# A fused attention and gated feed-forward kernel on one core: four blocks in every slot from the 22nd on, and the last output block in two halves

## The chip, the core and the metric

The kernel runs on one core of a Trainium2 chip. The metric is the device time of one execution in microseconds (us). Three runs of the kernel before the change gave 404.66, 405.2 and 404.98 us; their median is 404.98 us. The profile and the trace come from a further execution, which took 405.6 us.

## The reference, cut to what matters

Inputs q, k and v are float32 of shape (8 batches, 8 heads, 576 tokens, 64). Attention is computed twice and added: once over keys, queries and values averaged in groups of four tokens (144 of them), whose result is repeated four times, and once over a band in which a token sees only the keys less than 4 away. The sum, with the heads side by side, is x, 4608 tokens by 512. Then comes a gated feed-forward layer:

```python
out_up = np.repeat(sm_attn(q_d, k_d, v_d), 4, axis=2)      # q_d, k_d, v_d: means of 4 tokens
scores = np.where(abs(pos[:, None] - pos[None, :]) < 4, scale * q @ k.T, -1e9)
x = (out_up + softmax(scores) @ v)                         # as (4608, 512)
y = (np.maximum(x @ w_gate, 0) * (x @ w_val)) @ w_out      # 512 -> 1536 -> 512
```

## The kernel before, in words

**Two kinds of work are interleaved by hand.** The attention is done in 32 pairs of heads (pair p is two heads of batch p // 4). The feed-forward layer is cut into 9 chunks of 512 tokens. A chunk has twelve **h blocks** (`ffn_h`, 8 matmuls of 128x512 at line 588, then a Relu on ScalarE at line 596 and a product on VectorE at line 598 that makes the tile g) and four **y blocks** (`ffn_y`, 12 matmuls of 128x512 at line 604 into one PSUM bank, a copy to `y_sb` by ScalarE at line 612; `store_y` then issues the store from SyncE's queue, SP, at line 618).

**The list of blocks.** All of them stand in one list, `ffn`, three h blocks and then one y block of the chunk before, over and over, with the four y blocks of the last chunk at the end. `ffn_do` takes the first of the list. If it is an h block whose chunk needs tokens of a batch that isn't finished yet (`made`, the count of finished pairs, is too small), the call does nothing: a *blocked* call.

**The slots.** `slot(n)` for n from -2 to 33 writes out, in program order, the stages of several pairs and up to five calls of `ffn_do`; every engine then runs its own instructions in that order. For n from 14 on, in program order (line numbers of what is timed):

1. SP queue: the DMA transpose of the attention weights of pair n-1 (`turn_a`, line 505, tile `at`), of q and k of pair n+2 (`turn_qk`, line 268), loads of q and k of a pair five ahead (line 180) and of v of pair n+4 (lines 191 and 218), then the stores of finished y blocks.
2. The scores of pair n: TensorE (PE) at lines 336 and 353; VectorE (DVE) adds the mask (389), takes the maximum (411) and subtracts it (412, tile `sm`), and takes the maxima of the pooled scores (395, 396); ScalarE (ACT) the exponentials (448, 436). GpSimd (POOL) sums q and k in fours (323, 326).
3. First call of `ffn_do`.
4. Outputs of pair n-2 on PE: `u_ps` at line 532 and `o_ps` at 555, which read `at`; ACT copies `o_ps` (563). DVE does the sums and weights of pair n (453, 455, 460), and only then the addition that writes the tokens of pair n-2 into `xT` (`add_x`, line 572), after which `made` grows by one. POOL normalises the pooled weights (487).
5. Second call of `ffn_do`, casts on ACT and POOL, then the third and the fourth call, and the fifth where there is one.

Pair p of a batch fills the quarter p % 4 of the features of `xT`; the matmuls of an h block go through the quarters in order, so the fourth of each group of four reads what the last pair of the batch wrote. The matmul outputs `s_ps` (two), `h_ps` (two for each h block), `u_ps` (two), `o_ps` and `y_ps` take six PSUM banks in turn.

**The quota**, the number of calls, is 4 in even slots and 5 in odd ones from slot 14 to the end. Followed through the list, slots 22 to 33 make 54 calls, of which three are blocked: the first of slot 29 (chunk 6 waits for pair 27), the last of slot 32 and the first of slot 33 (chunk 7 waits for pair 31). After slot 33, 32 blocks are left and run one after the other; this is the tail.

Of the kernel before, what the change touches and what calls it, by code (L numbers as in the profile page):

```python
# [41 lines left out]
def _dap(t_ap: bass.AP, extra_off: int, dims) -> bass.AP:  # L42
    return bass.AP(tensor=t_ap.tensor, offset=t_ap.offset + extra_off, ap=list(dims))
# [3 lines left out]
def kernel(  # L47
# [10 lines left out]
    nc = tc.nc  # L58
# [3 lines left out]
    DM = H * D  # L62
    DF = w_gate.shape[1]
    NTOK = B * S
    TCH = 512
    NCH = NTOK // TCH
    NJJ = DF // 128
# [17 lines left out]
    wo_sb = wpool.tile([128, NJJ, DM], FP16, name="wo_sb")  # L85
# [54 lines left out]
    def bank(shape, name, dt=FP32):  # L140
        return psum.tile(shape, dt, name=name, tag="bank")


    def load_h_weights(i):
        cols = slice(384 * i, 384 * i + 384)
        for src, dst in ((w_gate, wg_sb), (w_val, wv_sb)):
            nc.gpsimd.dma_start(
                dst[:, :, cols],
                _dap(src, 384 * i, [[DF, 128], [128 * DF, 4], [1, 384]]),
            )  # L150

    def load_y_weights(i):
        nc.gpsimd.dma_start(
            wo_sb[:, 3 * i : 3 * i + 3, :],
            _dap(w_out, 3 * i * 128 * DM, [[DM, 128], [128 * DM, 3], [1, DM]]),
        )
# [4 lines left out]
    def load(p):  # L161
        off = 2 * p * S * D
        nat = p_nat.tile([96, 2, 768], FP32, name="nat", tag="nat")
        if p < NPE:


            t = nat.rearrange("p a c -> p (a c)").rearrange("p (b h c) -> p b h c", b=3, h=2)
            for src, r0, r1, blk, g0 in (
                (q, 0, 96, 0, 0),
                (q, 0, 48, 1, 96),  # L170
                (k, 48, 96, 1, 0),
                (k, 0, 96, 2, 48),
            ):
                nc.sync.dma_start(  # L174
                    t[r0:r1, blk],
                    _dap(src, off + 4 * g0 * D, [[4 * D, r1 - r0], [S * D, 2], [1, 4 * D]]),
                )
        else:
            for i, src in ((0, q), (1, k)):
                nc.sync.dma_start(  # L180
                    nat[:, i].rearrange("p (h j d) -> p h j d", h=2, j=6),
                    _dap(src, off, [[D, 96], [S * D, 2], [96 * D, 6], [1, D]]),
                )
        st[p] = dict(nat=nat)

    def load_v(p):
        off = 2 * p * S * D
        vst = v_t[p % NV]

        def win(rows, lo, par, w, nw):  # L190
            nc.sync.dma_start(
                vst[64 * par + lo : 64 * par + lo + rows, w : w + nw, :],
                _dap(
                    v,
                    off + (32 * (2 * w + par) - 3 + lo) * D,
                    [[D, rows], [64 * D, nw], [1, D]],
                ),
            )


        if p == 0:
            win(48, 0, 0, 1, NW - 1)
            win(45, 3, 0, 0, 1)
        else:
            win(48, 0, 0, 0, NW)
        if p == NP - 1:
            win(48, 0, 1, 0, NW - 1)
            nc.vector.memset(vst[96:VR, NW - 1, :], 0.0)
            win(35, 0, 1, NW - 1, 1)
        else:  # L210
            win(48, 0, 1, 0, NW)
        st[p]["vst"] = vst
# [40 lines left out]
    def cast_qk_act(p):  # L253
        cast_qk(p, 0)
# [174 lines left out]
    def exp_d(p, h):  # L429
        s = st[p]  # L430
        if h == 0:
            s["ed"] = p_ed.tile([80, 4, S // 4], FP16, name="ed", tag="ed")
            s["sd"] = p_st.tile([80, 4], FP32, name="sd", tag="sd")
        for c in range(2):
            i = 2 * h + c
            nc.scalar.activation(  # L436
                out=s["ed"][:, i, :],
                in_=s["dp"][h][:, c, :],
                func=AF.Exp,
                scale=SCALE / 16.0,  # L440
                bias=s["nb"][:, i : i + 1],
                accum_out=s["sd"][:, i : i + 1],
            )
# [136 lines left out]
    gts = {}  # L580
    ysb = []

    def ffn_h(c, jj):
# [14 lines left out]
        nc.vector.tensor_tensor(out=g, in0=r, in1=h2, op=ALU.mult)  # L598
        gts.setdefault(c, []).append(g)

    def ffn_y(c, ty):
        y = bank([128, DM], "y_ps")
        for jj in range(NJJ):
            nc.tensor.matmul(  # L604
                out=y,
                lhsT=gts[c][jj][:, bass.ts(ty, 128)],
                rhs=wo_sb[:, jj, :],
                start=(jj == 0),
                stop=(jj == NJJ - 1),
            )  # L610
        y_sb = p_y.tile([128, DM], FP32, name="y_sb", tag="y")
        nc.scalar.copy(out=y_sb, in_=y)  # L612
        ysb.append((c * TCH + ty * 128, y_sb))

    def store_y():
        while ysb:
            row, y_sb = ysb.pop(0)
            nc.sync.dma_start(_dap(out, row * DM, [[DM, 128], [1, DM]]), y_sb)

# [9 lines left out]
    def ffn_do():  # L631
        if ffn:
            t = ffn[0]
            if t and t[0] == "h" and made[0] < 4 * (min((t[1] + 1) * TCH - 1, NTOK - 1) // S + 1):
                return
            ffn.pop(0)
            if t:
                (ffn_h if t[0] == "h" else ffn_y)(t[1], t[2])
# [5 lines left out]
    def at_stage(p, *fs, pe=None):  # L644
        if 0 <= p < NP and (pe is None or pe == (p < NPE)):
            for f in fs:
                f(p)
# [5 lines left out]
    loaded = [0]  # L653

    def slot(n):
        quota = 0 if n < 4 else 3 if n < 14 else 5 if n % 2 else 4
        at_stage(n - 1, turn_a, pe=False)
        at_stage(n + 2, turn_qk, pe=False)
        while loaded[0] < min(NP, n + (5 if n < NPE - 2 else 6)):
            load(loaded[0])  # L660
            if loaded[0] < NPE:
                load_v(loaded[0])
            loaded[0] += 1
        at_stage(n + 4, load_v, load_v4, pe=False)
        store_y()
        at_stage(n, scores, scores_d)
        at_stage(n - 1, turn_en_pe, pe=True)
        at_stage(n, pool_v, mask_l, shift_l, copy_vd, exp_l, max_d)
        if n == 0:
            cast_qk_act(1)  # L670
        at_stage(n + 2, cast_qk_pool, pe=True)
        if n + 2 < NPP:
            at_stage(n + 2, cast_v, pe=True)
        at_stage(n + 1, pool_qk, pe=False)
        if n < 4 or n >= NPE:
            at_stage(n + 1, turn_qk_pe, pe=True)
        if quota > 1:
            ffn_do()
        if 4 <= n < NPE:
            at_stage(n + 1, turn_qk_pe, pe=True)  # L680
        at_stage(n - 1, turn_ad_pe, pe=True)
        at_stage(n, lambda p: exp_d(p, 0))
        at_stage(n - 1, outputs, pe=True)
        at_stage(n - 2, outputs, pe=False)
        at_stage(n, sums, weights_l)
        at_stage(n - 1, x_stage, pe=True)
        at_stage(n - 2, x_stage, pe=False)
        at_stage(n, lambda p: exp_d(p, 1))
        if n != -1:
            at_stage(n + 2, cast_qk_act, pe=True)  # L690
        if quota:
            ffn_do()
        if n + 2 >= NPP:
            at_stage(n + 2, cast_v, pe=True)
        at_stage(n + 1, pool_qk, pe=True)
        at_stage(n, weights_d)
        at_stage(n + 3, cast_qk_act, cast_qk_pool, pe=False)
        at_stage(n + 2, cast_v, sum_v4, pe=False)
        if 1 <= n < 5:
            load_h_weights(n - 1)  # L700
        elif 5 <= n < 9:
            load_y_weights(n - 5)
        if quota > 2:
            ffn_do()
        if quota > 3:
            ffn_do()
        if quota > 4:
            ffn_do()

    with tc.manual_schedule():  # L710
        for n in range(-2, NP + 2):
            slot(n)
        while ffn:
            ffn_do()
            store_y()
# [30 lines left out]
```

## Time and profile before

| | |
|---|---|
| median of three runs | 404.98 us (404.66 to 405.2) |
| the profiled execution | 405.6 us |
| its span, first to last instruction | 403.8 us |
| PE busy in the span | 373.0 us (92%) |
| DVE, ACT, POOL busy | 255.9, 206.0, 198.5 us |
| slot 22 begins (first scores of pair 22) | 210.96 us |
| slot 29 begins and ends | 282.88 and 298.94 us |
| PE's last matmul ends | 399.85 us |
| last copy of y on ACT begins | 399.91 us, 0.58 us long |

The span is a little shorter than the execution's time, by 1.8 us here; what lies around it is not in the trace. A row of the timeline gives start, length, engine, line and operation, and in brackets how long its engine was idle just before and what ended that. In the table of stretches, each engine has its busy time and its number of instructions, then the granted clock of PE (1.00 is full speed), the DMA share and the GB/s moved.

### The profile page before, as it was taken

The page shows a single profiled execution, that of the slowest core. Times are in us where ns is not written, and L with a number is a line of the kernel's source. Part 1 is how long each engine was busy: PE and PEld are TensorE (multiplying, and loading weights), DVE is VectorE, ACT ScalarE, POOL GpSimd, SP SyncE. Part 2 cuts the span into 40 slices and gives each one's busy share as a digit, 9 for nine tenths or more (in the row PEclk, how much of TensorE's full clock was granted, in tenths as well). Part 3 has the DMA queues.
Part 4 walks back from the last instruction along what each step waited for, and adds up shares of the span by engine and source line. Part 5 has one row for each costly group of instructions (what it writes and reads, how often), then busy time and mean ns, then how long its engine had stood idle before and what let it go on. Part 6 is the DMA issues. An engine that isn't in the chain of part 4 may idle for free.

```text
span 403.8 us, 11560 instructions
## 1 busy us (share of the span) xinstructions
PE 373.0 (92%) x4544; PEld 192.4 (48%) x4544; DVE 255.9 (63%) x640; ACT 206.0 (51%) x580; POOL 198.5 (49%) x248
## 2 busy tenths in 40 slices
PE   2699897898999999999999999999599999999996
PEld 2587465555544444444444444444244444444442
DVE  4788789878688868775767676777647532222210
ACT  3577577767575555555555555545335422332321
POOL 5587587755668776757475766564551100000000
PEclk9999999989899999999999999999799999999999
DMA  8999999997999999999999999999322100100112
GB/s 195 228 206 216 217 215 234 223 205 164 204 197 194 231 214 204 221 229 204 221 236 228 209 210 201 206 208 197 86 58 58 55 28 26 54 26 26 45 42 97
DMA packets 172059, 65.78 MB, mean 163 GB/s; under 512 B 152726, under 2 KB 165478, under 8 KB 172006
## 3 DMA queue, kind: packets, MB, share of 16 engines
q1 hardware_dynamic: 165830, 60.18, 75.9%
q0 software_dynamic: 5824, 4.72, 7.7%
q8 instruction: 35, 0.57, 0.6%
q10 hardware_dynamic: 352, 0.16, 0.2%
q14 instruction: 18, 0.15, 0.1%
HBM read 48.52 MB, written 9.44 MB: 144 GB/s over the span
## 4 chain that ended last, share of the span: by engine, by line
PE 71%; DMA 9%; DVE 8%; ACT 5%; issue 3%; SPq 2%; POOL 1%; POOLq 0%; ACTq 0%
PE h_ps L588 40%; PE y_ps L604 23%; DMA vst<-in_v_dram 8%; PE s_ps L336 2%; DVE sm L412 2%; PE u_ps L532 2%; DVE s_ps L389 1%; DVE mx L411 1%; PE d_ps L353 1%; SPq L174 1%; PE o_ps L555 1%; DMA nat<-in_k_dram 1%; DVE g L598 1%; ACT ed L436 1%; ACT r L596 1%
## 5 line engine op out<-in xcount | busy, mean ns | idle before, releaser
L598 DVE TENSOR_TENSOR g<-r,h_ps 128x512 f16<-128x512 f16 x108 | 73.9, 684 | 96.6 <-PE h_ps L588 75.2
L588 PE MATMUL h_ps<-xT,wg_sb 128*128 128x512 f16 x432 | 114.9, 388 | 5.5 <-DVE xT L572 4.5
L588 PE MATMUL h_ps<-xT,wv_sb 128*128 128x512 f16 x432 | 114.2, 388 | 0.2
L604 PE MATMUL y_ps<-wo_sb,g 128*128 128x512 f16 x432 | 99.2, 381 | 0.2 <-DVE sm L412 0.2
L596 ACT ACTIVATE r<-h_ps 128x512 f16<-128x512 f32 x108 | 64.3, 596 | 48.7 <-PE h_ps L588 48.4
L588 PEld LDWEIGHTS <-wv_sb 128*128 128x128 f16 x432 | 43.1, 100 | 59.6 <-issue 11.4
L604 PEld LDWEIGHTS <-g 128*128 128x128 f16 x432 | 41.8, 98 | 50.5 <-issue 1.4
L487 POOL TENSOR_TENSOR wts<-ed,rd 80x288 f16<-80x288 f16 x40 | 25.8, 664 | 76.4 <-ACT h L249 24.5
L588 PEld LDWEIGHTS <-wg_sb 128*128 128x128 f16 x432 | 39.1, 99 | 45.9 <-issue 2.9
L612 ACT COPY y_sb<-y_ps 128x512 f32<-128x512 f32 x36 | 21.0, 583 | 62.3 <-PE y_ps L604 62.1
L448 ACT ACTIVATE e<-sm 96x456 f16<-96x456 f32 x32 | 18.6, 583 | 57.1 <-DVE sm L412 57.0
L436 ACT ACTIVATE ed<-d_ps,nb 80x144 f16<-80x144 f32 x128 | 47.5, 380 | 0.0
L262 POOL CAST v<-vst 112x1152 f16<-112x1152 f32 x32 | 37.0, 1158 | 12.7 <-DMA vst<-in_v_dram 10.4
L323 POOL TENSOR_TENSOR t<-qkT 128x576 f32<-128x576 f16 x27 | 30.9, 1143 | 7.4 <-DVE qkT L293 7.4
L389 DVE TENSOR_TENSOR s_ps<-s_ps,mask_sb 96x228 f32<-96x228 f32 x64 | 22.1, 390 | 16.0 <-PE s_ps L336 16.0
L251 POOL CAST h<-nat 96x768 f16<-96x768 f32 x35 | 29.3, 836 | 5.4 <-DMA nat<-in_k_dram 4.8
L572 DVE TENSOR_TENSOR xT<-u_ps,od 128x288 f16<-128x288 f32 x64 | 26.0, 446 | 5.0 <-ACT od L563 5.0
L395 DVE TENSOR_REDUCE d_ps<-d_ps 80x2 f32<-80x288 f32 x64 | 28.9, 452 | 0.0
L412 DVE TENSOR_TENSOR sm<-s_ps,mx 96x228 f32<-96x228 f32 x64 | 25.1, 392 | 2.2
L249 ACT CAST h<-nat 96x768 f16<-96x768 f32 x29 | 24.2, 839 | 4.2 <-DMA nat<-in_k_dram 4.2
L436 ACT ACTIVATION_READ_ACCUMULATOR ed<-d_ps,nb 80x1 f32 x128 | 26.2, 204 | 0.0
L460 DVE TENSOR_TENSOR wts<-e,rl 96x456 f16<-96x456 f16 x32 | 24.8, 776 | 1.1
(53 smaller groups left out, 373.7 us busy)
## 6 DMA issues: line engine op xcount, KB each, us to landing
vst<-in_v_dram SPq DMA_DIRECT2D x62, 216.0 KB, 4.9
out_dram<-y_sb SPq DMA_DIRECT2D x36, 256.0 KB, 3.6
nat<-in_q_dram SPq DMA_DIRECT2D x20, 288.0 KB, 4.2
nat<-in_k_dram SPq DMA_DIRECT2D x20, 288.0 KB, 4.3
v<-in_v_dram SPq DMA_DIRECT2D x40, 144.0 KB, 4.4
nat<-in_q_dram SPq DMA_DIRECT2D x12, 192.0 KB, 7.2
nat<-in_k_dram SPq DMA_DIRECT2D x12, 192.0 KB, 5.1
wg_sb<-in_moe_w_gate_dram POOLq DMA_DIRECT2D x4, 384.0 KB, 8.6
```

Source lines behind the costliest of these rows:

```text
L251: nc.gpsimd.tensor_copy(out=dst, in_=src)
L262: nc.gpsimd.tensor_copy(out=s["v16"], in_=s.pop("vst"))
L323: nc.gpsimd.tensor_tensor(out=t1, in0=qkv[:, :, :, 0], in1=qkv[:, :, :, 1], op=ALU.add)
L389: nc.vector.tensor_tensor(out=sp, in0=sp, in1=mask_sb, op=ALU.add)
L395: nc.vector.tensor_reduce(out=nbr, in_=s["dp"][h], axis=AX.X, op=ALU.max)
L412: nc.vector.tensor_tensor(out=sm[:, half, :], in0=sp, in1=mx[:, half, None].to_broadcast([96, 6, 38]), op=ALU.subtract,)
L436: nc.scalar.activation(out=s["ed"][:, i, :], in_=s["dp"][h][:, c, :], func=AF.Exp, scale=SCALE / 16.0, bias=s["nb"][:, i : i + 1], accum_o ...
L572: nc.vector.tensor_tensor(out=x5[:, :, par], in0=up[par].rearrange("p l (t f) -> p l t f", f=4), in1=od4[:, :, par, :, None].to_broadcast( ...
L588: nc.tensor.matmul(out=h, lhsT=w[:, kk, bass.ts(jj, 128)], rhs=xT[:, kk, bass.ts(c, TCH)], start=(kk == 0), stop=(kk == 3),)
L596: nc.scalar.activation(out=r, in_=h1, func=AF.Relu)
L598: nc.vector.tensor_tensor(out=g, in0=r, in1=h2, op=ALU.mult)
L604: nc.tensor.matmul(out=y, lhsT=gts[c][jj][:, bass.ts(ty, 128)], rhs=wo_sb[:, jj, :], start=(jj == 0), stop=(jj == NJJ - 1),)
```

## The change

The fifth call of `ffn_do` is made only in odd slots up to 21, so slots 22 to 33 all make four calls. Followed through the list, none of the 48 calls is blocked any more, each slot holds three h blocks and one y block, in the order h, (outputs), h, y, h, and 35 blocks are left for the tail.

The y block of the last 128 tokens is computed in two halves of 256 columns: 12 matmuls of 128x256 and a copy by ACT, then 12 more into a second bank and a copy by DVE. Each half has a store of its own. All other y blocks are as before.

```diff
     def ffn_y(c, ty):
-        y = bank([128, DM], "y_ps")
-        for jj in range(NJJ):
-            nc.tensor.matmul(
-                out=y,
-                lhsT=gts[c][jj][:, bass.ts(ty, 128)],
-                rhs=wo_sb[:, jj, :],
-                start=(jj == 0),
-                stop=(jj == NJJ - 1),
-            )
+        row = c * TCH + ty * 128
+        last = row + 128 == NTOK
         y_sb = p_y.tile([128, DM], FP32, name="y_sb", tag="y")
-        nc.scalar.copy(out=y_sb, in_=y)
-        ysb.append((c * TCH + ty * 128, y_sb))
+        for i in range(2 if last else 1):
+            cols = slice(i * DM // 2, (i + 1) * DM // 2) if last else slice(0, DM)
+            y = bank([128, cols.stop - cols.start], "y_ps")
+            for jj in range(NJJ):
+                nc.tensor.matmul(
+                    out=y,
+                    lhsT=gts[c][jj][:, bass.ts(ty, 128)],
+                    rhs=wo_sb[:, jj, cols],
+                    start=(jj == 0),
+                    stop=(jj == NJJ - 1),
+                )
+            if i:
+                nc.vector.tensor_copy(out=y_sb[:, cols], in_=y)
+            else:
+                nc.scalar.copy(out=y_sb[:, cols], in_=y)
+            ysb.append((row, cols, y_sb))
...
-        quota = 0 if n < 4 else 3 if n < 14 else 5 if n % 2 else 4
+        quota = 0 if n < 4 else 3 if n < 14 else 5 if n < 22 and n % 2 else 4
```

`store_y` takes the columns with the row and stores them alone.

More of the change, by code (lines that the diff above doesn't have):

```diff
@@ L601, in ffn_y @@
     def ffn_y(c, ty):
-        y = bank([128, DM], "y_ps")
-        for jj in range(NJJ):
-            nc.tensor.matmul(
-                out=y,
-                lhsT=gts[c][jj][:, bass.ts(ty, 128)],
-                rhs=wo_sb[:, jj, :],
-                start=(jj == 0),
-                stop=(jj == NJJ - 1),
-            )
-        y_sb = p_y.tile([128, DM], FP32, name="y_sb", tag="y")
-        nc.scalar.copy(out=y_sb, in_=y)
-        ysb.append((c * TCH + ty * 128, y_sb))
+        row = c * TCH + ty * 128
+        last = row + 128 == NTOK
+        y_sb = p_y.tile([128, DM], FP32, name="y_sb", tag="y")
+        for i in range(2 if last else 1):
[14 more added lines that the diff above has]
+            ysb.append((row, cols, y_sb))
     def store_y():
         while ysb:
-            row, y_sb = ysb.pop(0)
-            nc.sync.dma_start(_dap(out, row * DM, [[DM, 128], [1, DM]]), y_sb)
+            row, cols, y_sb = ysb.pop(0)
+            n = cols.stop - cols.start
+            nc.sync.dma_start(
+                _dap(out, row * DM + cols.start, [[DM, 128], [1, n]]), y_sb[:, cols]
+            )
     ffn = []
```

## The prediction

> **What bounds the kernel now.** The page first: PE is busy 92% of the span, and the slices show where it isn't.
>
> ```profile
> PE   2699897898999999999999999999599999999996
> ...
> PEclk9999999989899999999999999999799999999999
> DMA  8999999997999999999999999999322100100112
> ```
>
> A slice is 10.1 us. From the eleventh on PE is full but for the last and the 29th (282.7 to 292.8 us), where its clock falls too. So from slot 22 on time is won or lost only where PE stands still or runs slow. Next, the stretches between the first scores of one pair and of the next (slots 22, 23, 25, 28, 29 and 30):
>
> ```profile
> 210.96:220.32 9.36, 9.36 (x126) 4.38 (x126) 7.23 (x19) 5.25 (x17) 4.69 (x7) 1.00 1.24 221
> 220.32:231.45 11.13, 11.09 (x134) 5.17 (x133) 7.91 (x20) 5.97 (x18) 8.16 (x11) 1.00 1.30 216
> ...
> 240.65:252.69 12.04, 11.15 (x134) 5.17 (x133) 8.00 (x20) 6.09 (x18) 8.79 (x11) 1.00 1.24 215
> ...
> 273.68:282.88 9.20, 9.20 (x126) 4.39 (x125) 7.20 (x19) 5.22 (x16) 3.94 (x6) 1.00 0.84 195
> 282.88:298.94 16.06, 11.94 (x125) 5.08 (x125) 7.52 (x19) 4.92 (x15) 10.48 (x13) 0.79 0.29 73
> 298.94:308.14 9.20, 9.20 (x125) 4.40 (x125) 7.20 (x19) 4.60 (x15) 1.29 (x2) 1.00 0.08 30
> ```
>
> Slots 28, 29 and 30 do the same work on PE (three h blocks of 1.73 us and a y block of 2.59, by the chain of waits, and the pair's matmuls), yet slot 29 takes 16.06 us instead of 9.20. PE's timeline says why:
>
> ```profile
> 283.79 0.37 PE L555 MATMUL o_ps<-at,vd 48*64 48x80 f16 x12
> 284.95 0.82 PE L588 MATMUL h_ps<-xT,wg_sb 128*128 128x512 f16 x3 [0.78 <-DVE sm L412]
> 289.10 0.58 PE L588 MATMUL h_ps<-xT,wg_sb 128*128 128x512 f16 x1 [3.33 <-DVE xT L572]
> 289.48 1.91 PE L588 MATMUL h_ps<-xT,wv_sb 128*128 128x512 f16 x4
> 291.19 1.91 PE L588 MATMUL h_ps<-xT,wg_sb 128*128 128x512 f16 x4
> 292.90 1.80 PE L588 MATMUL h_ps<-xT,wv_sb 128*128 128x512 f16 x4
> 294.53 1.03 PE L588 MATMUL h_ps<-xT,wg_sb 128*128 128x512 f16 x4
> ```
>
> The first call was blocked, so outputs follow scores at once and the next h block, the first of chunk 6, needs pair 27's addition, which DVE does behind pair 29's mask, maxima and weights. PE stands some 4.2 us (0.87, then 3.33 in front of the fourth matmul). Then 13 matmuls begin 0.42 us apart (289.10 to 294.53) instead of 0.216: half clock, 13 x 0.2 = 2.6 us more. 4.2 + 2.6 = 6.8, which is 16.06 - 9.20.
>
> **Removed by the quota.** (a) Slot 29: the block there is now the tenth h block of chunk 5, which needs nothing of pair 27, and chunk 6 begins with the slot's last block: **6.86 us**. What is late next? In slot 23, whose first four blocks lie as they will in slot 29, `xT` is done 7.0 us after the slot's start (DVE 226.50 + 0.81 less 220.32); the matmul that needs it comes after scores 0.6, h 1.8, outputs 0.6, h 1.9, y 2.6 and three matmuls 0.65, at 8.2. So 1.2 us to spare. (b) Slot 25 takes 12.04; slot 21 with the same five blocks takes 10.93: 1.11 us lost, 0.65 of it before the matmul that needs pair 23's `xT`. In the new order one more h block stands ahead of it: **1.11**. (c) Slot 33: the wait for pair 31 (0.51 before 327.80). Two blocks now lie between: **0.51**. Sum **8.48 us**. Work is only moved: three net blocks go to the tail, where PE already runs h and y blocks at 1.73 and 2.59 us with no idle row.
>
> **Added by the quota: a PSUM bank.** A slot takes twelve banks of six, so the slot's second h block meets the banks of the second score tile and of its first h block. Slots 22 and 23 already have the new order (an h block ends the slot before; then h, outputs, h, y):
>
> ```profile
> 223.37 1.04 PE L588 MATMUL h_ps<-xT,wg_sb 128*128 128x512 f16 x4
> 224.45 1.02 PE L588 MATMUL h_ps<-xT,wv_sb 128*128 128x512 f16 x4
> ```
>
> Four matmuls take 0.87, here the next four begin after 1.08: the bank is free when ACT's Relu of the first h block has ended (223.82 + 0.58), which stands behind the exponential, the subtraction and the mask, and the mask behind the g of the block before. Slots 22 and 23 lose 0.16 and 0.20 (9.36 - 9.20, 11.13 - 10.93). Slots 24 to 31 would now all be of this kind, where 24, 26, 27, 28 and 30 lose nothing today: 8 x 0.18 = **1.44 us**. Bounds: 0 (slot 21, with no h before it) and 0.46 a slot (slot 25, where that g came 0.4 later: 1.11 - 0.65), so 0 to 3.7.
>
> **Added by the quota: the DMA queue's pace.** Loads and transposes go through SP, with the DMA share above 1.2 until slot 27. Slots last 9.38 now, not 10.2 in the mean. The weights' transpose was issued so:
>
> ```profile
> 254.49 1.40 SPq L505 DMA_TRANSPOSE at<-wts  x1
> ...
> 264.92 1.32 SPq L505 DMA_TRANSPOSE at<-wts  x1
> ...
> 273.59 1.34 SPq L505 DMA_TRANSPOSE at<-wts  x1
> ```
>
> These are pairs 25, 26 and 27. POOL's weights of pair 26 were done at 261.0, SP came 3.9 us later and between issues it has no gap over 0.2 us: it is paced by the transfers, not by the engines, about 10.2 us a pair. If that pace holds whatever PE does, pair 26 lands at 264.92 + 6.8 (its landing time in the DMA view) = 271.7. Slot 28 would begin at 220.32 + 5 x 9.38 = 267.2 and want it 2.4 later (outputs at 222.76 in slot 23): 269.6. That is **2.0 us late**; pairs 24 and 25 come 0.2 and 0.5 early, and after slot 28 no loads are left. If SP follows PE (of 13 intervals before, four lasted 9.2 to 9.5 us; slot 21 moved 240 GB/s), it costs nothing. Behind the waiting `u_ps` all of PE stands, so a wait counts in full. No row decides; the middle, **1.0 us**, bounds 0 and 2.0.
>
> **The last block in halves.** Matmuls of 256 columns aren't in the trace. 512 take 0.216, so half is 0.108, and 24 of them 2.59 as before, plus perhaps 0.03. Against that stand 24 weight loads instead of 12; the row for a load is 98 ns. Were the 12 extra ones not hidden: 1.18 us. The nearest row is `v_ps` at line 369: eight matmuls of 128 columns, each with its own load, from 106.17 to 106.71, 67 ns each, so loads of 98 ns overlap. I take 0.03. The copy: ACT's 512 columns take 0.58; DVE takes 0.55 for 384 columns from PSUM (line 293) and 0.41 for 288 (half of line 572's 0.81), so about 0.4 for 256: 0.18 won, between 0.03 (the 384 row) and 0.24 (half of line 598's 0.68). The store: issued at 400.52, its data moves at 406 GB/s around 401.5 to 402.0, some 0.65 us for 256 KB; half is 0.3 less, bounds 0 and 0.35. The first half's copy and store run beside the second half's 1.3 us of matmuls. Together **0.45 us** won (loss of 1.15 to gain of 0.6).
>
> [...]
>
> **Sum.** -8.48 + 1.44 + 1.0 - 0.45 = -6.5 us. The profiled execution, 405.6 (span 403.8), would become 399.1 (397.3); it lies 0.6 above the median of the runs, so the median 404.98 becomes **398.5 us**. Bounds: all gains and no cost, 404.98 - 8.48 - 0.6 = 395.9; 3.7, 2.0 and no gain at the end, 402.2.
>
> **Rivals.**
> 1. *Transfers hold PE at more than one slot.* If landings also slow down while transfers are denser (7.0 and 7.2 us are the longest now), slots 26, 27 and 28 wait, 3 to 4 us in all: about 401.5. For it: the share above 1.2, SP without gaps. Against it: no wait of PE on a DMA between 185 and 335 us today.
> 2. *Weight loads show in the halves*, 1.2 us more: 399.7.
> 3. *The blocked wait only moves*: pair 27's `xT` is late for chunk 6 again. It needs DVE 1.2 us later than in slot 23; slot 25 had it 0.4 later. Were it as late as 2.5 us, PE would stand 1.3: 399.8.
> 4. *Slower.* One long wait in slot 28 and the clock. Slot 29 shows that 4.2 us of standing, with 0.8 us of work in between, brings half clock and 2.6 us more. Without the DMA term the change wins 7.5; a wait w in front of `u_ps` costs w + 2.6 once w is about 3.3, and decides from w = 5 on, that is when pair 26 lands 3 us later than at the old pace. At w = 6: 404.98 - 7.5 + 8.6 = 406.1. Against it: the longest landing adds only 0.2 to the 6.8 used.
> 5. *Neither cost appears* (SP follows, the Relu comes in time): 404.98 - 8.48 - 0.45 = 396.1.
>
> [...]
>
> **Chances.** Forecast (397 to 401) 0.66, rival 1 0.12, rival 2 0.04, rival 3 0.03, rival 4 0.04, rival 5 0.11. The range 396.0 to 402.2 takes in the cost bounds and leaves out rival 4, part of rival 1 and the best of rival 5. A measurement of this kernel tells about 0.2% (0.8 us) from no change; no case but rival 4 and its neighbours comes near: faster 0.95, same 0.01, slower 0.04.
>
> **What would show it.** Right: slot 29 at about 9.4 us at clock 1.00, slots 24 to 31 at 9.3 to 9.5 with 0.15 to 0.2 between the second h block's two groups, the gap in front of pair 23's and pair 31's `xT` gone, DVE's copy near 0.4. The DMA term shows as idle time before `u_ps` in slots 27 or 28, ended by a DMA of `at`. Wrong: a second stretch at half clock, a wait on `xT` in slot 29, or slots over 9.6 us.

## The result, and the profile after

The changed kernel takes **398.96 us** (median of four runs, 398.57 to 399.48) against 405.09 us for the kernel before (four runs): a ratio of 0.9851, 95% interval 0.9834 to 0.9868. The forecast was 398.5 us. The profiled execution took 398.91 us, its span 397.1 us, 6.7 us less than before. In the medians and ratios below, executions over 1.5% above the fastest of their kernel are left out; the traces of e2 (granted clock 0.95 in the mean) and of e8 are of such executions.

The page's slices, as before: the hole in the 29th slice is gone, on PE and in its clock.

```profile
PE   2699988888999999999999999999999999999996
...
PEclk9999999989999999999999999999999999999999
DMA  7999999998999999999999999999322100100112
```

The stretches from one pair's first scores to the next, of slots 22 to 25 and 27 to 30 (PE, weight loads, DVE, ACT and POOL busy, PE's clock, DMA share, GB/s):

```profile
210.72:220.08 9.36, 9.36 (x125) 4.38 (x124) 7.22 (x19) 5.26 (x17) 4.69 (x7) 1.00 1.22 218
220.08:229.49 9.41, 9.37 (x127) 4.40 (x126) 7.22 (x19) 5.33 (x17) 6.45 (x9) 1.00 1.16 229
229.49:238.89 9.40, 9.36 (x126) 4.39 (x126) 7.23 (x19) 5.32 (x17) 6.46 (x9) 1.00 1.11 239
238.89:248.29 9.40, 9.35 (x125) 4.39 (x125) 7.22 (x19) 5.31 (x17) 6.46 (x9) 1.00 1.16 229
...
257.69:268.11 10.42, 9.60 (x125) 4.46 (x124) 7.46 (x20) 5.32 (x17) 6.46 (x9) 1.00 1.23 216
268.11:277.51 9.40, 9.36 (x125) 4.39 (x124) 7.22 (x19) 5.32 (x17) 6.46 (x9) 1.00 1.11 195
277.51:286.94 9.43, 9.39 (x126) 4.39 (x126) 7.23 (x19) 4.61 (x16) 6.49 (x9) 1.00 0.41 113
286.94:296.36 9.42, 9.38 (x125) 4.36 (x124) 7.22 (x19) 4.60 (x16) 5.36 (x7) 1.00 0.23 62
```

Slot 29 (277.51) lasts 9.43 us where it lasted 16.06, at full clock. The slots from 23 on last 9.40 to 9.43, 0.2 more than slots 28 and 30 did before. One doesn't fit: slot 27, at 257.69, lasts 10.42, and nothing in the prediction says so. PE's timeline of slot 29 has no idle time in front of the first h block of chunk 6, at 285.12:

```profile
280.26 0.37 PE L555 MATMUL o_ps<-at,vd 48*64 48x80 f16 x12
280.57 1.04 PE L588 MATMUL h_ps<-xT,wg_sb 128*128 128x512 f16 x4
281.65 1.02 PE L588 MATMUL h_ps<-xT,wv_sb 128*128 128x512 f16 x4
282.53 2.75 PE L610 MATMUL y_ps<-wo_sb,g 128*128 128x512 f16 x12
285.12 1.03 PE L588 MATMUL h_ps<-xT,wg_sb 128*128 128x512 f16 x4
```

The second and third rows begin 1.08 us apart where four matmuls take 0.87: the gap at the PSUM bank, in each slot now.

What happens in slot 27 stands in DVE's timeline (in brackets: idle before, and what ended it):

```profile
257.87 0.69 DVE L598 TENSOR_TENSOR g<-r,h_ps 128x512 f16<-128x512 f16 x1 [1.91 <-ACT vd L425]
259.31 0.11 DVE L208 MEMSET vst<- 16x64 f32 x1 [0.76 <-POOL v L262]
259.35 0.70 DVE L389 TENSOR_TENSOR s_ps<-s_ps,mask_sb 96x228 f32<-96x228 f32 x2
```

For pair 31 alone, `load_v` has DVE write zeros into 16 rows of a `vst` buffer (line 208), in the program order of slot 27 ahead of that pair's mask. The buffer is free when POOL has cast pair 28's v out of it, a cast that POOL runs at the end of slot 26's list. DVE stands 0.76 us before 0.11 us of work, the mask begins 1.66 us after the slot's start where it begins 0.78 after it in slot 26, and with it the subtraction that frees PSUM: PE waits 0.36 before `o_ps` and 0.34 before `h_ps`. Counted from the slot's start, the outputs' `o_ps` begins 0.52 us later than in slot 29, the second h block 0.94 and its second group 1.01, which is what the slot is longer.

The issues of the weights' transposes of pairs 25, 26 and 27:

```profile
252.87 2.01 SPq L505 DMA_TRANSPOSE at<-wts  x1
...
262.68 1.81 SPq L505 DMA_TRANSPOSE at<-wts  x1
...
271.00 1.33 SPq L505 DMA_TRANSPOSE at<-wts  x1
```

They come 9.8 and 8.3 us apart; PE's waits from 185 us on name no DMA. At the end come the second half's copy and, in the DMA view, the time from issue to landing of a half's store (2.0 us for a whole block before):

```profile
393.74 0.42 DVE L618 COPY y_sb<-y_ps 128x256 f32<-128x256 f32 x1 [12.28 <-DMA out_dram<-y_sb]
```

```profile
out_dram<-y_sb SPq DMA_DIRECT2D x1, 128.0 KB, 1.7
```

The DMA named in the copy's bracket ended 0.04 us before the copy began, but ACT had been writing to the same tile since 392.42. PE's last matmul ended at 393.65, 0.09 us before the copy; in e2, where that gap is 0.10, the bracket names PE. So the copy most likely waited for PE. From the last matmul to the end of the span some 3.5 us pass, 4.0 before.

### The profile page after: what moved, and what is told of

Same layout as the page of the kernel before. It is cut to its first block, busy times and chain, and to the rows that moved or that the text cites. A ratio compares the mean times of both kernels' runs of the same rounds, so it can differ in the third digit from the quotient of the medians.

```text
span 397.1 us, 11602 instructions
## 1 busy us (share of the span) xinstructions
PE 371.2 (93%) x4556; PEld 192.9 (49%) x4556; DVE 256.1 (64%) x641; ACT 205.6 (52%) x580; POOL 198.0 (50%) x248
## 4 chain that ended last, share of the span: by engine, by line
PE 64%; DMA 9%; DVE 9%; ACT 7%; issue 4%; POOL 3%; SPq 3%; ACTq 0%; POOLq 0%; DVEq 0%
PE h_ps L588 36%; PE y_ps L610 23%; DMA vst<-in_v_dram 6%; ACT r L596 3%; DMA nat<-in_k_dram 3%; DVE sm L412 3%; DVE s_ps L389 2%; SPq L174 2%; DVE mx L411 2%; PE s_ps L336 1%; DVE g L598 1%; PE o_ps L555 1%; PE d_ps L353 1%; PE u_ps L532 1%; POOL h L251 1%
## 5 line engine op out<-in xcount | busy, mean ns | idle before, releaser
L588 PE MATMUL h_ps<-xT,wg_sb 128*128 128x512 f16 x432 | 113.7, 386 | 0.5 <-DVE sm L412 0.5
L588 PE MATMUL h_ps<-xT,wv_sb 128*128 128x512 f16 x432 | 112.6, 383 | 0.6
L610 PE MATMUL y_ps<-wo_sb,g 128*128 128x512 f16 (+1 forms) x444 | 98.5, 373 | 0.0
L610 PEld LDWEIGHTS <-g 128*128 128x128 f16 x444 | 43.1, 98 | 49.2
L620 ACT COPY y_sb<-y_ps 128x512 f32<-128x512 f32 (+1 forms) x36 | 20.8, 579 | 57.9 <-PE y_ps L610 57.8
```

The lines of the kernel that those rows point to most:

```text
L588: nc.tensor.matmul(out=h, lhsT=w[:, kk, bass.ts(jj, 128)], rhs=xT[:, kk, bass.ts(c, TCH)], start=(kk == 0), stop=(kk == 3),)
L610: nc.tensor.matmul(out=y, lhsT=gts[c][jj][:, bass.ts(ty, 128)], rhs=wo_sb[:, jj, cols], start=(jj == 0), stop=(jj == NJJ - 1),)
```

## The experiments

The time before slot 14 differs by some us from run to run with the first loads: the first scores of pair 14 come at 128.9 us in the trace of the kernel before and at 125.2 in one of a kernel (e6) with the same program up to there. So beside the ratios, which have wide intervals on some chips, this table gives the time **from the first scores of slot 21 to the end of the span**, which leaves that out. It is read from one trace of each kernel, and the spans are given to 0.1 us.

| kernel | ratio to before (95% interval) | slot 21 to end, us | against before |
|---|---|---|---|
| before | | 203.77 | |
| the change | 0.9851 (0.9834 to 0.9868) | 197.31 | -6.46 |
| e10: the same again | 0.9857 (0.9810 to 0.9905) | 197.33 | -6.44 |
| e1: quota alone | 0.9874 (0.9833 to 0.9916) | 197.87 | -5.90 |
| e2: halves alone | 1.0016 (0.9984 to 1.0047) | | |
| e3: zeros by POOL | 0.9804 (0.9761 to 0.9847) | 196.46 | -7.31 |
| e4: five blocks only to slot 20 | 0.9831 (0.9789 to 0.9872) | 195.83 | -7.94 |
| e5: e3 and e4 together | 0.9819 (0.9780 to 0.9859) | 197.57 | -6.20 |
| e6: before, slot 27 with four | 0.9869 (0.9822 to 0.9916) | 198.85 | -4.92 |
| e7: before, slots 25 and 27 with four | 0.9863 (0.9820 to 0.9907) | 198.13 | -5.64 |
| e8: three blocks in slots 20 to 26 | 1.0144 (1.0083 to 1.0205) | | |
| e9: e5 with fewer loads | 0.9745 (0.9695 to 0.9795) | 194.58 | -9.19 |

**e1 and e2: each part alone.** e1 makes `last` always false; e2 has the new `ffn_y` with the old quota.

```diff
-        last = row + 128 == NTOK
+        last = False
```

> The new quota with the last block whole, as before. If the quota is what won and the halves are worth the 0.5 us that the two traces show at the end (3.97 against 3.45 us from the last matmul to the end of the span), this takes about 399.5 us: slot 29 lasts 9.4 us at clock 1.00, slot 27 again 10.4, and 3.9 to 4.0 us lie behind the last matmul. If the halves had won more than that, it takes 400 or more.

> The last block in halves with the quota of before. If the halves only shorten the end, it takes 404.5 us: slot 29 keeps its 16 us with half clock behind it, and about 3.45 us lie behind the last matmul; the 24 matmuls of the halves take 2.6 us. If weight loads showed in the halves, they would take up to 3.8 us and the whole 405.5.

e1 took 399.1 us. Slot 27 lasts 10.42 again, 4.0 us lie behind the last matmul where the change has 3.5, and slot 21 to the end is longer by about as much: the quota brings some 5.9 of the 6.46, the halves the rest. In e2's trace the wait of slot 29 stays, 3.20 us before the matmul that needs pair 27's `xT`. e2's time (404.40 against 403.84 for before on that chip) can't tell a gain of 0.5 from none; the halves' worth rests on e1 against the change.

**e3: the zeros by another engine.**

```diff
-            nc.vector.memset(vst[96:VR, NW - 1, :], 0.0)
+            nc.gpsimd.memset(vst[96:VR, NW - 1, :], 0.0)
```

> The changed kernel with one instruction on another engine: the zeros in the last rows of v of pair 31 (line 208) are written by GpSimd, which makes the value that VectorE waited for there, instead of by VectorE. Theory: slot 27's 10.42 us come from VectorE standing 0.76 us in front of this write, with the mask behind it; it falls to 9.4 and the time to about 398.0. Rival: in slot 27 a transfer would be late anyway (the old pace of the queue); then a wait before u_ps takes its place and the time stays at 398.9.

Slots 27 and 28, and PE in slot 28:

```profile
256.65:266.06 9.41, 9.38 (x126) 4.40 (x126) 7.22 (x19) 5.33 (x17) 6.67 (x10) 1.00 1.04 229
266.06:275.61 9.55, 9.27 (x125) 4.39 (x125) 7.25 (x19) 5.32 (x17) 6.62 (x9) 1.00 1.15 175
```

```profile
268.85 0.46 PE L532 MATMUL u_ps<-at,v 38*64 38x32 f16 x36 [0.28 <-DMA at<-wts]
```

Slot 27 falls from 10.42 to 9.41, so VectorE's wait in front of the zeros was its 1.0 us. The rival holds a little too: pair 26's transpose, hidden behind the lost microsecond in the changed kernel, is now 0.28 us late. Net 0.85 us.

**e4: a y block at each slot's end.**

```diff
-        quota = 0 if n < 4 else 3 if n < 14 else 5 if n < 22 and n % 2 else 4
+        quota = 0 if n < 4 else 3 if n < 14 else 5 if n < 21 and n % 2 else 4
```

> The changed kernel with five blocks only up to slot 20: one block less before slot 22, so every slot from 21 on runs h, outputs, h, h, y and ends with a y block. Theory: the 0.2 us of each slot come from the Relu of the first h block, late because the mask stands behind the g of an h block that ended the slot before; with a y block there the slots last 9.2 us instead of 9.4, and ten of them win 1.6 to 2.0 us; slot 27 still loses 0.6 to 1.0 for the zeros. About 397.1. Rival: four blocks a slot are as fast as the transfers allow (the queue took 9.8 us a pair in slots 24 to 26), so waits on DMA take the place of the gaps: slots of 9.4 us, 398.5 to 399.

Slots 25, 26, 27 and 28, and what they wait for:

```profile
236.07:245.30 9.23, 9.23 (x127) 4.41 (x126) 7.20 (x19) 5.24 (x16) 6.54 (x9) 1.00 1.19 220
245.30:254.64 9.34, 9.26 (x125) 4.39 (x124) 7.20 (x19) 5.24 (x16) 6.63 (x9) 1.00 1.16 234
254.64:264.86 10.22, 9.50 (x125) 4.38 (x124) 7.34 (x20) 5.24 (x16) 6.30 (x9) 1.00 1.16 235
264.86:274.26 9.40, 9.27 (x125) 4.40 (x125) 7.33 (x19) 5.23 (x16) 6.63 (x9) 1.00 1.27 209
```

```profile
PE u_ps L532 <- DMA at<-wts: 0.4, 1, 0.4
PE h_ps L588 <- DVE sm L412: 0.2, 1, 0.2
```

Slots 21 to 24 last 9.20 each and slot 25 9.23: with a y block in front of the scores the gap inside the second h block is gone, and the block that moved to the tail costs no more there than its own time. Slot 27 loses 1.0, for the zeros and a wait of 0.43 on pair 25's transpose. From slot 21 on, about 1.5 us are won over the change, where 1.6 to 2.0 were expected.

**e5: both.**

> Both repairs in one kernel: five blocks only up to slot 20, and the zeros of pair 31 written by GpSimd. Theory: slots of 9.2 us, nothing lost for the zeros, and what is left is the pace of the transfers, which already showed as waits of 0.28 us (slot 28) and 0.43 us (slot 27) before u_ps in the two runs that had one repair each; here it is 0.5 to 1.5 us in slots 26 to 28 together. Span about 394.3 us, some 2.8 below the changed kernel. Rival: the transfers give no more than one of the repairs won, waits of 2 us or more come, span 396 or above.

PE in slots 26, 27 and 28:

```profile
248.88 0.46 PE L532 MATMUL u_ps<-at,v 38*64 38x32 f16 x36 [0.63 <-DMA at<-wts]
...
259.05 0.47 PE L532 MATMUL u_ps<-at,v 38*64 38x32 f16 x36 [0.90 <-DMA at<-wts]
...
269.19 0.46 PE L532 MATMUL u_ps<-at,v 38*64 38x32 f16 x36 [0.87 <-DMA at<-wts]
```

With 0.54 in slot 25, 2.9 us of waits; slots 25 to 28 last 9.8 to 10.2, slots 21 to 24 still 9.20. For the 0.54 the profile names DVE, but pair 23's transpose, issued at 232.05, landed 6.9 us later, at 238.95, 0.03 us before that `u_ps`. The theory was wrong here and the rival right: from slot 21 on, this trace with both repairs is no shorter than those of the change, which has neither. The transposes of pairs 20 to 26 were issued 10.1 us apart in this run, 9.8 with the change (10.0 in e10).

**e8: how fast the transfers go.** The quota is 3 in slots 20 to 26.

> The changed kernel with three blocks instead of four in slots 20 to 26, so that PE's own work in them takes 6.4 to 7.4 us. It asks how fast the transfers can go. Theory: loads, transposes and stores of a pair take at least about 9.3 us, so with the 4 to 5 us of lead used up PE waits before u_ps or s_ps for DMAs, 2 us a slot in slots 23 to 27, 6 to 9 us in all, perhaps with half clock; time 405 or more, above before. Rival: the queue follows PE, as it did from 10.2 to 9.8 us a pair; slots of 7.5 us and a time near 399.

```profile
215.92:227.15 11.23, 9.18 (x119) 4.11 (x118) 8.27 (x19) 4.54 (x15) 7.80 (x11) 0.85 1.16 209
227.15:235.11 7.96, 6.67 (x113) 3.21 (x113) 6.92 (x18) 5.46 (x17) 5.26 (x7) 1.00 1.18 210
235.11:247.18 12.07, 9.01 (x117) 4.25 (x117) 6.71 (x18) 4.95 (x16) 7.14 (x10) 0.86 1.26 211
```

```profile
220.49 0.46 PE L532 MATMUL u_ps<-at,v 38*64 38x32 f16 x36 [2.06 <-DMA at<-wts]
...
221.23 1.89 PE L588 MATMUL h_ps<-xT,wg_sb 128*128 128x512 f16 x4
...
241.54 0.67 PE L532 MATMUL u_ps<-at,v 38*64 38x32 f16 x36 [3.06 <-DMA at<-wts]
...
242.53 1.89 PE L588 MATMUL h_ps<-xT,wg_sb 128*128 128x512 f16 x4
...
260.79 0.46 PE L532 MATMUL u_ps<-at,v 38*64 38x32 f16 x36 [2.62 <-DMA at<-wts]
...
262.69 1.91 PE L588 MATMUL h_ps<-xT,wv_sb 128*128 128x512 f16 x4
```

The shorter executions took 409.31 and 411.85 us, 1.4% more than before. The three stretches are slots 23 to 25. PE waits 10.9 us for transposes in slots 22 to 27, and with three of the waits (2.06, 3.06 and 2.62 us) comes half clock: four matmuls in 1.7 us instead of 0.87. Slots 21 to 27 last 10.0 us in the mean, and the transposes of pairs 20 to 26 were issued 10.0 us apart, though PE's own work in a slot fills about 7. So here the transfers set the pace and not PE; it is 9.8 to 10.3 us a pair over these seven transposes in the traces of before, the change, e1, e3, e4, e5, e8 and e10.

**e9: fewer bytes.** `load_v4` returns ahead of its two DMAs for pairs 24 to 31.

```diff
         st[p]["v4"] = v4 = v4_t[p % NV]
+        if p >= 24:
+            return
```

> The kernel with both repairs, without the second load of v (288 KB a pair of some 2.2 MB that a pair moves) for pairs 24 to 31, issued in slots 20 to 27; the four-token sums of v of these pairs are then made from what the buffer held. Theory: the waits of 2.9 us before u_ps with both repairs are the bandwidth of the transfers, 9.8 to 10.1 us a pair; with 13% less to move a pair takes about 8.6 us, the waits go, slots 21 to 31 last 9.2 us, and from the start of slot 21 to the end of the span 194.5 us pass (197.6 with both repairs, 203.8 before). Rival: the waits are the latency of the transposes or SP's own issuing; then most of the 2.9 us stay.

```profile
235.42:244.62 9.20, 9.20 (x126) 4.38 (x126) 7.20 (x19) 5.22 (x16) 6.46 (x9) 1.00 1.12 231
244.62:253.82 9.20, 9.20 (x126) 4.40 (x126) 7.20 (x19) 5.22 (x16) 6.46 (x9) 1.00 1.07 226
253.82:263.02 9.20, 9.20 (x126) 4.40 (x126) 7.20 (x19) 5.22 (x16) 6.65 (x10) 1.00 0.87 181
```

Slots 25 to 27 of 9.20 us, no wait of PE behind 195 us, 194.58 us to the end where 194.5 was expected; the transposes of pairs 21 to 24 were issued 8.4 us apart. The transfers moved 231 and 226 GB/s in slots 25 and 26 of e9, and 190, 249 and 216 in slots 25 to 27 of e5: fewer bytes at about the same rate. e9 also takes two issues a pair from the SP queue, whose rows lasted 0.8 to 1.4 us together, so it doesn't part the bytes from the issues. That the bytes held e5 back is likely, not shown: the shortest rows of all issues of a pair add up to some 6.5 us, well under 8.4.

**e6 and e7: the blocked wait by degrees.** The kernel before, with four blocks in slot 27 alone, or in 25 and 27.

```diff
-        quota = 0 if n < 4 else 3 if n < 14 else 5 if n % 2 else 4
+        quota = 0 if n < 4 else 3 if n < 14 else 5 if n % 2 and n not in (25, 27) else 4
```

> The kernel before with four blocks instead of five in slot 27 alone. Slot 29 then begins with a y block that can run, so y, outputs, and at once the first h block of chunk 6. Theory: its fourth matmul is reached 4.5 us after the slot's start and xT is done at 6.4, so PE stands about 1.9 us instead of 4.2 in two pieces; if a stretch of 1.9 us leaves the clock alone, slot 29 (five blocks, 10.93 without loss) lasts 12.8 us and the time is 5 us below before. Rival: any wait on xT there brings the half clock, then 2.6 us more, slot 29 at 15.4 and only 2.3 us won.

> The kernel before with four blocks instead of five in slots 25 and 27 alone. Slot 29 then runs h, outputs, y, and the first h block of chunk 6. Theory: its fourth matmul is reached 6.3 us after the slot's start, xT is done at about 7.0, so PE stands 0.7 us, slot 29 lasts 11.6 us at clock 1.00 and the time is 6 us below before: two of the six dropped fifth calls bring nearly all. Slot 25 still loses some 0.7 to 1.1. Rival: the gain comes from shorter slots as such, a third of it for a third of the dropped calls, 2 us below before.

Slot 29 of e6, and the matmul in it that needs pair 27's `xT`; then the same of e7:

```profile
276.57:290.07 13.50, 11.95 (x137) 5.57 (x136) 8.00 (x20) 4.62 (x15) 9.24 (x11) 1.00 0.40 105
```

```profile
282.86 0.38 PE L588 MATMUL h_ps<-xT,wg_sb 128*128 128x512 f16 x1 [1.55 <-DVE xT L572]
```

```profile
276.44:288.11 11.67, 11.09 (x134) 5.18 (x133) 8.00 (x20) 5.37 (x17) 8.85 (x12) 1.00 0.45 119
```

```profile
283.49 0.38 PE L588 MATMUL h_ps<-xT,wg_sb 128*128 128x512 f16 x1 [0.58 <-DVE xT L572]
```

No block in front of the dependent one cost 6.86 us; one y block leaves 1.55, an h block, outputs and a y block leave 0.58, both at full clock. (e6's slot holds two y blocks, so its 13.50 would be 11.79 without loss, as in slot 27 before, not the 10.93 of the expectation.) One of the six dropped fifth calls brings 4.92 us and two bring 5.64: not shorter slots as such, but which block stands first in slot 29.

**e10: the change again.**

> The changed kernel once more, beside the run above and on its chip, to see which figures hold from run to run. Theory: what is fixed by the order of the program holds to 0.05 us (9.40 us a slot, 10.4 for slot 27, 186.4 us from slot 22's start to the end of the span), the time before slot 14 moves by a few us with the first loads, and no wait of PE on a DMA appears from slot 22 on. Rival: the lead of the transfers was luck, and a wait of 0.3 us or more before u_ps appears in slots 26 to 28.

Slot 27 lasts 10.42 and 197.33 us pass from slot 21 on; from slot 22 it is 186.4, as expected, and PE waits for no DMA.

## Why the prediction was right

By slot 21 to end the change won 6.46 us; the sum had 6.5. Term by term:

1. *Slot 29's block order, 6.86.* Right: 16.06 became 9.43, and 0.2 of that is the bank term. e6 and e7 show that it hangs on what stands in front of chunk 6's first block, and that the half clock goes with the long wait: it came with 3.33 us, and at 1.55 (e6) and 0.58 (e7) the granted clock was 1.00.
2. *Slots 25 and 33, 1.11 and 0.51.* Right: no wait of PE on `xT` is left from slot 22 on.
3. *A PSUM bank, 1.44 (0 to 3.7).* Right: 0.20 a slot, 1.6 in all, and e4 removes it by a y block at each slot's end, as slots 28 and 30 had it before. That the Relu frees the bank is read from the times (the next matmul begins 0.05 us after it); no run separated bank and Relu.
4. *The DMA queue's pace, 1.0 (0 to 2.0).* **Wrong for this kernel**: PE waits for no DMA. The step that failed is that pair 26 lands at 271.7 and is wanted at 269.6. Its transpose was issued at 262.68 and landed 6.5 later, at 269.2, since the pace of pairs 20 to 26 was 9.8 and not 10.2; and slot 28 wanted it 2.44 after 268.11, at 270.55, because slot 27 had lost 1.0 us (term 5). The pace alone doesn't explain it: in e1, with the same quota, it was 10.2 and PE didn't wait either. Counted from the start of slot 21, pair 26's transpose was issued after 62.9 us here, 63.8 in e10, 63.5 in e1 and 64.6 in e3, with the same blocks up to there, and after 64.9 before. So that this term came to nothing is in part luck, and the lost microsecond of slot 27 helped. The mechanism is real and near: 0.28 us in e3, where that microsecond is gone, 0.4 in e4, 2.9 in e5.
5. *What was missed: the zeros of pair 31, 1.02.* The question of what is late next was put for `xT` alone, not for DVE's other waits. The waits view of before had the line:

```profile
DVE vst L208 <- POOL v L262: 0.2, 1, 0.2
```

   A fifth of a microsecond there. POOL's cast ended 1.0 us after slot 27's start before (261.74 + 1.14 less 261.89) and ends 1.6 after it now (258.10 + 1.15 less 257.69), since in the new order of slot 26 the pooled weights ahead of it on POOL begin 7.8 us into the slot instead of 7.05; 0.2 became 0.76. That the sum came out is luck in this: two errors of 1 us, terms 4 and 5, cancel. Without the wait for the zeros (e3) 7.31 us are won, 0.8 more than the sum.
6. *The halves, 0.45.* Right: about 0.5. The copy takes 0.42 (0.4 forecast), the store lands 0.3 us sooner, and the last y block, 391.04 to 393.65, takes 2.6 us, as one of 12 matmuls did. Twelve more weight loads of 98 ns that nothing hid would have cost 1.2 us by the prediction's estimate; the trace doesn't show it.

The rivals: the first is wrong for this kernel and right for e5. The second and third didn't come; pair 27's `xT` was done 7.0 us after slot 29's start and read 1.3 us later, as forecast. The fifth came by half, for the DMA cost and not for the bank. The fourth's mechanism is e8's: waits on a transpose that also take the clock, slower than before; but the price that it set, half clock only from a wait of 3.3 us, was too lenient, since 2.06 us were enough there.

e3, e4 and e5 take less than before, and on these chips 395.9, 397.2 and 397.8 us, where the changed kernel took 399.3 beside e9; their intervals overlap one another and its own. From slot 21 on, e4's trace is the shortest of a kernel that computes everything; e3's is 0.6 us longer.

## What to carry to other kernels

The more work the order puts between a value and its reader, the shorter the reader's engine waits (3.33 us in slot 29 before, 1.55 in e6, 0.58 in e7): look at the first block after each gate, not at the number of blocks, and price the half clock together with the wait (2.6 us beside 4.2 in slot 29 before). When a bound goes, list every wait of the engines that feed the one that ran ahead, the short ones of 0.2 us too, and ask how each moves in the new order. A queue that runs late but in step with the kernel can be at its own limit: here a pair took it some 10 us, its lead hid that at the change's slots of 9.4 us, and with both repairs (e5, slots of 9.2 us up to slot 24) PE waited 2.9 us and nothing was won over the change until a load was left out (e9).

## What the runs showed of the hardware

PE's clock fell to half at shorter idle stretches than the prediction's price took (about 3.3 us): in e8 at waits of 2.06, 3.06 and 2.62 us, and not at 1.55 (e6) or 1.29 (e8). It was half for some 3.4 to 3.5 us each time, an estimate from the granted clock of the three slots (0.85 over 11.23 us, 0.86 over 12.07 and 0.87 over 13.57). In slot 29 before, 13 matmuls over 5.4 us ran at half clock after the wait of 3.33.

From pair 20's transpose to pair 26's, the loads, transposes and stores of a pair, some 2.2 MB, took 9.8 to 10.3 us in the traces of before, the change, e1, e3, e4, e5, e8 and e10, at 216 GB/s before and 227 with the change; 10.0 us also in e8, where PE's own work left room for 7.
